# Sliding-window attention feeding a squared-ReLU MLP: three 64-query strips of scores a block instead of four quarters, half blocks of two batches merged, and a new instruction order

## The chip, the cores and the metric

One core of a Trainium2 chip. The time is that of one execution on the device, in microseconds. The engines named below are TensorE (PE, matmuls; its weight loads are shown as PEld), VectorE (DVE), ScalarE (ACT), GpSimd (POOL) and SyncE (SP); the last two, and ACT now and then, also issue DMA transfers.

## The reference

Attention with 8 batches, 8 heads, 576 positions and head size 64. A query sees itself and the 127 positions before it, with a linear bias that depends on the head. The result, as a 4608 x 512 matrix, goes through an MLP of width 2048 with relu squared.

```
B, H, S, D = q.shape                       # 8, 8, 576, 64
window = 128
scores = (q @ k^T) / sqrt(D)
rel = pos[:, None] - pos[None, :]
bias = slopes[h] * -abs(rel)
mask = (rel >= 0) & (rel < window)
scores = where(mask, scores + bias, -1e9)
attn = softmax(scores)
x = (attn @ v) laid out as (B * S, H * D)  # 4608 x 512
h = x @ w_in                               # 512 x 2048
out = relu(h) ** 2 @ w_out                 # 2048 x 512
```

## The kernel before

**Blocks.** A batch's 576 positions are cut into blocks of 128 (`kb` 0 to 3) and a half block of 64 (`kb` 4, `HALF`). `seq` lists the blocks, 40 of them; `ranges` lists 36 column ranges of 128 tokens, where the half blocks of two batches share one. A *job* makes the attention of one or two blocks: six jobs of kind "diag" (`kb` 0: four of a single block, made by `lone`, and two of two blocks), 24 of kind "full" (one block with the block before it) and four of kind "half" (the half blocks of two batches, each with its batch's block 3 before it).

**A full job.** Keys lie on partitions and queries on columns. The scores of a head are two 128 x 128 matmuls over 64 rows of contraction (`pieces`): the block before's keys against the block's queries, and the block's own keys. Heads come in pairs, r = 0 on partitions 0 to 63 and r = 1 on 64 to 127. The 16 matmuls of line 974 fill four PSUM banks of two heads x 256 columns. Four `ACTIVATE` of line 1001 take the exponentials of 512 columns each into a buffer `Pt` (three of them, tag "P"), laid out [128 keys, 8 heads, 2 parts, 128 queries]. Four products of line 1009 on DVE multiply with `masks`, which hold the bias's exponential and zeros outside the window. So of each 256 x 128 window of keys and queries all four quarters of 64 queries are computed, the parts outside the window too. Then `values` multiplies: for each half of the heads eight matmuls of line 1089 (4 heads x 2 parts, 65 columns: 64 of v and one of ones for the sum), a reciprocal (line 1108), and a normalisation (line 1117) into a buffer of x. A DMA transpose on SP (line 1127) puts x into `xT`.

**A half job.** Each of the two half blocks is loaded (lines 854 and 859: k, q and v, 64 rows each) into buffers of its own, transposed by its own DMA transpose on SP (line 900), and has its own 16 score matmuls of 64 columns. The unused half of key rows is zeroed where a buffer is used first (`zero`, line 787). The four exponentials and the four products (line 1016) cover both blocks. Then each block has its own 16 PV matmuls, two reciprocals and two normalisations of 64 rows.

**The MLP.** Tokens go in nine groups of 512. The first product is line 1241 for groups 0 to 2 (`unit`), line 1259 for groups 3 to 5 (`fc_step`) and line 1340 for groups 6 to 8, which use seven products of half-size blocks instead of eight. Relu is line 1202 on ACT, squaring line 1214 on DVE or line 1212 on ACT. The second product is line 1416 for group 0 and line 1503 for the rest, again with seven products (`product`, p = 1 to 7), whose sums of operands DVE makes (`prepare`, line 1633). Outputs are stored by DMA from SP.

**Order.** Nothing here is ordered by dependence alone. Every step is a `Task` with a key, costs and dependencies; `Plan.order` goes through them with a model of engines, buffers and transfers and writes out one fixed order per engine. `ADJ` adds a number to the key of nearly every task, and `SLACK` and the `lat` and `dma` arguments say how late the plan counts on a transfer. The order is fixed before the program runs, so an engine that waits for something holds up all that stands behind it. The rings of buffers ("kq" 4, "v" 9, "kqT" 7, "P" 3, "x" 6, four PSUM banks "a") set how far steps can run ahead.

The plan gives a full job's scores this cost, and the loop over heads is this:

```
t = plan.add({"PE": 213.0 + len(grps) * 2 * len(pieces) * mm(128 if n == 128 else 64)}, due - 32, scores, ...
for c0, w, part, mk, mq in pieces:
    for r in range(2):
        rows = slice(64 * r, 64 * r + 64)
        nc.tensor.matmul(sS[2 * g2 + r].tile[:, jj * 256 + c0:jj * 256 + c0 + w],
                         tile_of(s_kqT[mk])[rows, c, :], tile_of(s_kqT[mq])[rows, C + c, 0:w], ...)
```

Of the kernel before, what the change touches and what calls it, by code (L numbers as in the profile page):

```python
# [11 lines left out]
AF = mybir.ActivationFunctionType  # L12
# [14 lines left out]
SLACK = {"kq": 0.0, "kqT": 4500.0, "v": 2000.0, "x": 2500.0}  # L27
# [11 lines left out]
G_STR = 1  # L39
G_A = 8  # L40
# [14 lines left out]
    "S1.1.0": 6358.822602, "S1.1.1": 6898.050375, "S1.2.0": 10041.2788363, "S1.2.1": 8169.065299, "S1.3.0":  # L55
    10013.995535, "S1.3.1": 8382.076385, "S1.4.0": 17801.930821, "S1.4.1": 15031.337, "S1.5.0": 17384.9929746,
    "S1.5.1": 20260.6174285, "S1.6.0": 22555.8403789, "S1.6.1": 21998.8655, "S1.7.0": 20043.5527584, "S1.7.1":
    25127.1329917, "S1.8.0": 25946.836, "S1.8.1": 26588.9614497, "S2.1.0": 4101.7175, "S2.1.1": 6358.118102,
    "S2.2.0": 8496.8719291, "S2.2.1": 10040.2218363, "S2.3.0": 13560.1077472, "S2.3.1": 12657.244, "S2.4.0":
    16530.7475695, "S2.4.1": 17130.93, "S2.5.0": 17756.8905682, "S2.5.1": 18438.1734398, "S2.6.0":  # L60
    23791.1643648, "S2.6.1": 22459.22941, "S2.7.0": 25315.958184, "S2.7.1": 24765.864872, "S2.8.0":
    24647.825372, "S2.8.1": 26728.7553177, "S3.1.0": 7691.34905, "S3.1.1": 5640.9850318, "S3.2.0": 9443.1491067,
    "S3.2.1": 8550.2682395, "S3.3.0": 10012.235035, "S3.3.1": 13110.8827156, "S3.4.0": 17415.1131664, "S3.4.1":
    18868.3965004, "S3.5.0": 16780.7561245, "S3.5.1": 19805.6045037, "S3.6.0": 22056.5286414, "S3.6.1":
    22074.9870258, "S3.7.0": 25314.861684, "S3.7.1": 26475.2942403, "S3.8.0": 24251.003782, "S3.8.1":
    28098.8773389, "S4.1.0": 6868.250375, "S4.1.1": 7190.2430892, "S4.2.0": 18682.0508077, "S4.2.1":
    18759.5925752, "S4.3.0": 16445.569448, "S4.3.1": 12628.3175, "S4.4.0": 16501.5050695, "S4.4.1":
    14245.0103734, "S4.5.0": 18363.1661199, "S4.5.1": 18363.1046199, "S4.6.0": 22239.6313394, "S4.6.1":
    20124.3504497, "S4.7.0": 26035.141, "S4.7.1": 24736.958872, "S4.8.0": 24185.8589207, "S4.8.1":
    26559.0364497, "b0": 100510, "b1": 100646.465, "b2": 100667.43, "b3": 100715.863, "c11.6.0": 18332.2568341,  # L70
    "c11.6.1": 19590.2485357, "c11.6.2": 21992.696259, "c11.6.3": 19462.4798324, "c11.7.0": 22016.1567401,
    "c11.7.1": 24935.5551633, "c11.7.2": 24734.8259005, "c11.7.3": 23120.6715, "c11.8.0": 26072.1522676,
    "c11.8.1": 26386.3929546, "c11.8.2": 24734.034331, "c11.8.3": 24615.9810863, "c11_1": 4307.4524817, "c11_2":
    8422.0862025, "c11_3": 14308.2115, "c11_4": 17422.5279746, "c11_5": 20884.9988781, "c11_6": 22886.3042408,
    "c11_7": 25714.9587071, "c11_8": 26289.7634823, "c12.6.0": 17228.9717667, "c12.6.1": 18740.1705159,
    "c12.6.2": 23047.354399, "c12.6.3": 25227.0637252, "c12.7.0": 21920.6848572, "c12.7.1": 20046.3418068,
    "c12.7.2": 26385.7442101, "c12.7.3": 21830.9803572, "c12.8.0": 21690.5237178, "c12.8.1": 24263.1766392,
    "c12.8.2": 22834.1277424, "c12.8.3": 24959.2783489, "c12_1": 4613.490023, "c12_2": 13092.42675, "c12_3":
    17664.7600933, "c12_4": 17114.3773214, "c12_5": 22247.0763394, "c12_6": 23129.1952857, "c12_7":
    26163.0233491, "c12_8": 27958.2748967, "c21.0.0_8": 24932.018008, "c21.1.0_8": 26617.6848177, "c21.1.128_8":  # L80
    24928.082008, "c22.6.0": 17468.542771, "c22.6.1": 22092.8820972, "c22.6.2": 22129.5325649, "c22.6.3":
    21949.9206161, "c22.7.0": 21925.0530715, "c22.7.1": 25171.6485544, "c22.7.2": 24892.6130205, "c22.7.3":
    26804.1028891, "c22.8.0": 24693.1109434, "c22.8.1": 25047.3577759, "c22.8.2": 26343.5233117, "c22.8.3":
    27112.1616464, "c22_1": 4337.716, "c22_2": 9783.687498, "c22_3": 11828.507, "c22_4": 17129.2863214, "c22_5":
    22020.5445824, "c22_6": 24970.1156274, "c22_7": 28091.4763389, "c22_8": 27264.6796621, "ck0": 9000458,
    "cq0": 9000504, "dist0": 100701.629, "dist1": 9000167, "e0.0": 100865.465, "e0.1": 100982.763, "e1.0":
    100912.829, "e1.1": 100971.528, "e10.0": 6024.8369206, "e10.1": 6023.9689206, "e10.2": 5839.0722412,
    "e10.3": 5838.2427412, "e11.0": 8333.0698163, "e11.1": 5840.1446162, "e11.2": 11096.131875, "e11.3":
    6021.8962956, "e12.0": 8273.2926913, "e12.1": 9520.9182666, "e12.2": 8282.49653, "e12.3": 8270.2366913,
    "e13.0": 13841.648643, "e13.1": 8283.554405, "e13.2": 11150.984125, "e13.3": 12454.1255232, "e14.0":  # L90
    8210.136138, "e14.1": 8787.0007703, "e14.2": 9519.8080166, "e14.3": 9466.008375, "e16.0": 8885.7162151,
    "e16.1": 8884.6537151, "e16.2": 10342.0834936, "e16.3": 10693.54, "e17.0": 8885.8656867, "e17.1":
    11233.30575, "e17.2": 12129.232199, "e17.3": 12189.03225, "e18.0": 15565.7505509, "e18.1": 15564.6630509,
    "e18.2": 12189.933125, "e18.3": 8882.9630617, "e19.0": 15661.0022219, "e19.1": 12190.774, "e19.2":
    11232.1335, "e19.3": 12188.795, "e2.0": 100934.863, "e2.1": 100993.562, "e20.0": 13016.628, "e20.1":
    14291.5031517, "e20.2": 15562.071875, "e20.3": 15561.406875, "e21.0": 11975.2805813, "e21.1": 13721.9226948,
    "e21.2": 11976.1653893, "e21.3": 15413.6828378, "e22.0": 14172.4779017, "e22.1": 14182.1584369, "e22.2":
    14418.4875177, "e22.3": 14169.3539017, "e24.0": 14226.6730813, "e24.1": 14727.898453, "e24.2":
    15627.3818759, "e24.3": 14602.2, "e25.0": 16482.863696, "e25.1": 13955.27798, "e25.2": 18313.139696,
    "e25.3": 14180.2126869, "e26.0": 14656.6730692, "e26.1": 18194.2829996, "e26.2": 13834.5302836, "e26.3":  # L100
    15828.1824093, "e27.0": 16758.2565536, "e27.1": 15940.2024397, "e27.2": 19504.1119452, "e27.3":
    15938.2764397, "e28.0": 15322.144554, "e28.1": 17988.7125373, "e28.2": 17767.8699853, "e28.3": 15319.004554,
    "e29.0": 15790.0544683, "e29.1": 15788.4093405, "e29.2": 15320.067929, "e29.3": 15786.4843405, "e3.0":
    101062, "e3.1": 101120.698, "e30.0": 15672.7835671, "e30.1": 17466.9708932, "e30.2": 18063.8736786, "e30.3":
    15666.3157155, "e32.0": 19352.6183651, "e32.1": 15668.3965905, "e32.2": 18682.2837426, "e32.3":
    17356.0710976, "e33.0": 18654.8004269, "e33.1": 15203.5509286, "e33.2": 15202.6409286, "e33.3":
    20451.1293954, "e34.0": 15669.9384683, "e34.1": 19765.183, "e34.2": 21275.2451008, "e34.3": 21274.3261008,
    "e35.0": 18534.8561769, "e35.1": 18461.4868024, "e35.2": 20490.0989946, "e35.3": 20336.2020638, "e36.0":
    19373.2814934, "e36.1": 20514.3671669, "e36.2": 20332.1955204, "e36.3": 23191.326944, "e37.0": 18603.768303,
    "e37.1": 21299.7554555, "e37.2": 24035.5923691, "e37.3": 24034.7217238, "e38.0": 21208.26042, "e38.1":  # L110
    24045.6924324, "e38.2": 24871.760639, "e38.3": 19778.8989624, "e4.0": 103407.667, "e4.1": 103466.365,
    "e4.2": 103513.063, "e4.3": 103559.762, "e6.0": 103674.667, "e6.1": 103733.365, "e6.2": 103780.063, "e6.3":
    103826.762, "e8.0": 5554.0984829, "e8.1": 7285.886, "e8.2": 5552.1759829, "e8.3": 5551.0879829, "e9.0":
    5928.4081491, "e9.1": 6031.827125, "e9.2": 6738.730625, "e9.3": 8390.4300663, "ev0.0.0": 100713.333,
    "ev0.0.2": 100713.333, "ev0.1.0": 100759.333, "ev0.1.2": 100785.733, "ev1.0.0": 100757.965, "ev1.0.2":
    100757.965, "ev1.1.0": 100780.298, "ev1.1.2": 100784.364, "ev2.0.0": 100713.43, "ev2.0.2": 100713.43,
# [481 lines left out]
def kernel(  # L598
# [23 lines left out]
    for b in range(0, B, 2):  # L622
        for x in [(b + i, kb) for i in range(2) for kb in range(1, HALF)]:
            jobs.append(("full", [len(seq)]))
            seq.append(x)
            ranges.append([x])
        jobs.append(("half", [len(seq), len(seq) + 1]))
        seq += [(b, HALF), (b + 1, HALF)]

        ranges.insert(len(ranges) - (b + 2 == B), seq[-2:])  # L630
# [1063 lines left out]
```

## Time and profile before

| | |
|---|---|
| median of 3 runs | 299.22 us (297.59 to 299.52) |
| the profiled execution's own time | 299.3 us |
| its span, first to last instruction | 297.4 us |
| mean granted TensorE clock | 1.00 |
| PE / PEld busy | 285.0 / 224.4 us |
| DVE / ACT / POOL busy | 244.0 / 205.8 / 106.3 us |
| line 974, scores of full, half and two-block diag jobs | 544 matmuls |
| line 1001, their exponentials | 120, 63.8 us, mean 604 ns |
| line 1089, PV | 576 matmuls |
| line 900, DMA transposes of q and k on SP | 32, median issue 1342 ns |
| DMA engines | 90% busy or more in the first 28 of 40 slices (to 208 us) |

A busy PE in this profile is one that has matmuls in flight; the matmul's mean duration (273 ns for 256 columns) holds the way through the array as well, so neighbours overlap and the rate is read from the distance of their starts. The chain that ended last is a list of pieces in order of time: start, length, engine and line, number of instructions. A wait is put down to what ended it.

### The profile page before, as it was taken

What the parts mean: (1) busy time and instruction counts of PE and PEld (TensorE: products, weight loads), DVE (VectorE), ACT (ScalarE), POOL (GpSimd) and SP (SyncE); (2) the same over time, 40 slices, a digit from 0 to 9 for tenths busy, and PEclk for the clock granted to TensorE, in tenths of its full rate; (3) what the DMA queues carried; (4) which work ended last, traced back from release to release, by engine and by line L of the source; (5) the groups of instructions that cost most, each with busy time, mean ns of one, the idle gap of its engine ahead of it and who ended that gap; (6) DMA issues with size and microseconds to landing.
All of it is one profiled execution on the core that took longest, in us unless ns stands there. A gap on an engine that the chain in (4) does not pass through costs nothing.

```text
span 297.4 us, 8313 instructions
## 1 busy us (share of the span) xinstructions
PE 285.0 (96%) x3279; PEld 224.4 (75%) x3299; DVE 244.0 (82%) x626; ACT 205.8 (69%) x392; POOL 106.3 (36%) x132
## 2 busy tenths in 40 slices
PE   7899999999998999899999999999999999999994
PEld 3588757888887986457656756768889888888884
DVE  5566568689976996689958997999999998799964
ACT  2785555495496655877679797878999578989600
POOL 8944488452842755441439622710000000000000
PEclk9999999999999999999999999999999999999999
DMA  9999999999999999999999999998212111201124
GB/s 125 168 201 207 184 180 173 155 157 174 163 165 186 161 146 182 158 165 139 155 186 150 148 191 169 165 130 171 68 40 79 53 35 37 71 2 35 31 77 144
DMA packets 170792, 39.62 MB, mean 133 GB/s; under 512 B 156800, under 2 KB 170240, under 8 KB 170752
## 3 DMA queue, kind: packets, MB, share of 16 engines
q0 software_dynamic: 115184, 18.10, 88.9%
q1 hardware_dynamic: 54768, 20.33, 40.0%
q10 hardware_dynamic: 800, 0.66, 0.8%
q8 instruction: 26, 0.43, 0.6%
q14 instruction: 14, 0.11, 0.1%
HBM read 36.70 MB, written 9.44 MB: 155 GB/s over the span
## 4 chain that ended last, share of the span: by engine, by line
PE 69%; DMA 14%; DVE 6%; POOL 4%; issue 3%; ACT 1%; SPq 0%; POOLq 0%; DVEq 0%
PE o L1503 25%; PE h L1259 12%; PE h L1340 10%; PE h L1241 8%; DMA vt<-in_v_dram 5%; PE o L1416 5%; DMA w_out_sb<-in_moe_w_out_dram 4%; PE pv L1089 4%; PE s L974 4%; DMA kqT<-kq 3%; DMA xT<-x 3%; POOL kq L854 2%; POOL vf L859 1%; DVE g L1214 1%; POOL w_in_sb L799 1%
## 5 line engine op out<-in xcount | busy, mean ns | idle before, releaser
L1202 ACT ACTIVATE rt<-h 128x512 bf16<-128x512 f32 (+1 forms) x109 | 64.8, 597 | 32.8 <-PE h L1241 13.9
L1001 ACT ACTIVATE P<-s 128x512 bf16<-128x512 f32 x120 | 63.8, 604 | 7.8 <-PE s L974 7.7
L1503 PEld LDWEIGHTS <-g 128*128 128x128 bf16 x624 | 59.9, 98 | 8.4
L1214 DVE TENSOR_TENSOR g<-rt 128x512 bf16<-128x512 bf16 (+1 forms) x100 | 41.4, 417 | 20.0 <-ACT rt L1202 18.6
L854 POOL DMA_DIRECT2D kq<-in_k_dram x39 | 33.1, 849 | 66.0 <-DMA kqT<-kq 60.7
L1503 PE MATMUL o<-w_out_sb,g 128*128 128x256 bf16 x384 | 47.5, 273 | 0.0
L1241 PE MATMUL h<-xT,w_in_sb 128*128 128x128 bf16 (+1 forms) x512 | 46.2, 246 | 1.0 <-DMA xT<-x 0.9
L1259 PE MATMUL h<-xT,w_in_sb 128*128 128x512 bf16 x178 | 45.5, 379 | 0.7
L1241 PEld LDWEIGHTS <-w_in_sb 128*128 128x128 bf16 x512 | 38.7, 98 | 5.2 <-issue 1.1
L1009 DVE TENSOR_TENSOR P<-P,masks 128x512 bf16<-128x512 bf16 x96 | 38.4, 417 | 2.5 <-ACT P L1001 0.7
L854 POOL DMA_DIRECT2D kq<-in_q_dram x39 | 33.3, 853 | 7.4 <-PE h L1241 3.1
L1117 DVE TENSOR_TENSOR x<-pv,rec 128x256 bf16<-128x256 f32 (+1 forms) x80 | 32.2, 416 | 0.9
L1503 PE MATMUL o<-wsum,sums 128*128 128x256 bf16 x256 | 31.6, 273 | 1.1 <-DVE osb L1561 0.6
L859 POOL DMA_DIRECT2D vt<-in_v_dram x32 | 27.0, 858 | 11.6 <-PE pv L1089 9.8
L1503 PE MATMUL o<-wsum,g 128*128 128x256 bf16 x240 | 29.8, 273 | 0.1
L1089 PEld LDWEIGHTS <-P 128*128 128x128 bf16 x576 | 24.0, 98 | 7.2 <-issue 2.0
L1259 PEld LDWEIGHTS <-w_in_sb 128*128 128x128 bf16 x192 | 16.9, 97 | 15.9
L1212 ACT ACTIVATE g<-rt 128x512 bf16<-128x512 bf16 x45 | 27.9, 629 | 1.1
L1503 PEld LDWEIGHTS <-sums 128*128 128x128 bf16 x256 | 24.4, 98 | 4.8 <-DVE sums L1633 0.6
L1361 DVE TENSOR_TENSOR vf<-h,vf 128x512 f32<-128x512 f32 x36 | 24.1, 683 | 0.8 <-ACT vf L708 0.4
L1202 ACT ACTIVATE rt<-vf 128x512 bf16<-128x512 f32 x36 | 22.2, 624 | 2.4 <-DVE vf L1361 2.2
L1089 PE MATMUL pv<-vt,P 128*128 128x65 bf16 x448 | 22.0, 193 | 1.3 <-DMA vt<-in_v_dram 1.3
(81 smaller groups left out, 382.0 us busy)
## 6 DMA issues: line engine op xcount, KB each, us to landing
out_dram<-osb SPq DMA_DIRECT2D x53, 128.0 KB, 3.8
kq<-in_k_dram POOLq DMA_DIRECT2D x31, 128.0 KB, 7.6
kq<-in_q_dram POOLq DMA_DIRECT2D x31, 128.0 KB, 7.9
vt<-in_v_dram POOLq DMA_DIRECT2D x24, 128.0 KB, 8.0
w_out_sb<-in_moe_w_out_dram POOLq DMA_DIRECT2D x4, 512.0 KB, 14.7
w_in_sb<-in_moe_w_in_dram POOLq DMA_DIRECT2D x3, 512.0 KB, 10.7
vf<-in_v_dram POOLq DMA_DIRECT2D x8, 128.0 KB, 6.9
out_dram<-osb SPq DMA_DIRECT2D x4, 256.0 KB, 6.4
```

Source lines behind the costliest of these rows:

```text
L854: nc.gpsimd.dma_start(view(kq[s_kq[m].idx], i), source(src, m, split))
L859: nc.gpsimd.dma_start(tile_of(s_v[m])[0:n, :, 0:D], source(v, m))
L1001: nc.scalar.activation(flat(Pt[sP.idx]), sS[i].tile.rearrange("p (j t) -> p j t", j=2)[:, :, lo:hi], AF.Exp, bias=0.0, scale=scale)
L1009: nc.vector.tensor_tensor(flat(Pt[sP.idx]), flat(Pt[sP.idx]), flat(masks), op=ALU.mult)
L1089: nc.tensor.matmul(sv.tile[0:full, hi * (D + 1):(hi + 1) * (D + 1)], prob, tile_of(s_v[mk])[:, h, 0:D + 1], start=mk == parts[0][1], stop= ...
L1117: nc.vector.tensor_tensor(o, heads(sv)[rows, :, 0:D], sr.tile[rows, :].unsqueeze(2).to_broadcast([n, 4, D]), op=ALU.mult)
L1202: nc.scalar.activation(srt.tile[:, 0:n], i, AF.Relu, bias=0.0, scale=1.0)
L1214: nc.vector.tensor_tensor(o, i, i, op=ALU.mult)
L1241: nc.tensor.matmul(slot.tile[:, f * w:(f + 1) * w], w_in_sb[:, cc, fc * 128:(fc + 1) * 128], xT[:, cc, lo % (XR * 128):lo % (XR * 128) + w ...
L1259: nc.tensor.matmul(slot.tile, w_in_sb[:, cc, fc * 128:(fc + 1) * 128], xT[:, cc, g * 512 % (XR * 128):g * 512 % (XR * 128) + 512], start=c ...
L1340: nc.tensor.matmul(slot.tile[:, j * 256:j * 256 + 256], a, b_, start=fresh and j == 0 and c == 0, stop=c == 1, skip_group_check=True)
L1503: nc.tensor.matmul(slot.tile[:, z * 256:z * 256 + 256], stationary(c), moving(c), start=fresh and z == 0 and c == 0, stop=c == F - 1, skip ...
```

## The change

Scores of a full block are now three strips of 64 queries per head. Strip one is the block before's 128 keys against the early 64 queries, strip two the block's own 128 keys against the late 64 queries. The third strip holds two 64 x 64 tiles on top of each other: the block's early keys with its early queries on partitions 0 to 63, and the block before's late keys with its late queries on partitions 64 to 127. The quarter that is left out in each part lies wholly outside the window. Two PSUM banks per r hold 512 and 256 columns. Exponentials are taken of these, 512 and 256 columns twice. Of the four mask products, the odd ones read the third strip once for each of the two quarters that it belongs to and multiply with masks whose other half is zero.

The half blocks of two batches are one block of 128 rows: one entry in `seq` (36 instead of 40), one kq buffer, one transpose, one key block for PV. Its scores are again two strips from 128 keys and one from 64 x 64 tiles. The exponentials lie in one P buffer, and a second one, `sR`, holds the late queries' share of the second batch's earlier block, with zeros (`clear`, `far_late`, `far_early`, `near`) where batch and query do not belong together. PV takes three parts a head and 128 queries at once.

Heads are laid out in P as even heads, then odd heads (`place`), as the single-block jobs had them. The plan's numbers for transfers and for the scores change (`S_PE`, `lat`, `SLACK`, `dma`), a few dependencies are added, and all of `ADJ` is replaced.

```diff
-SLACK = {"kq": 0.0, "kqT": 4500.0, "v": 2000.0, "x": 2500.0}
+SLACK = {"kqT": 4500.0, "v": 2300.0, "x": 2700.0}
+S_PE = 375.0
 ADJ = {
...
-        jobs.append(("half", [len(seq), len(seq) + 1]))
-        seq += [(b, HALF), (b + 1, HALF)]
+        jobs.append(("half", [len(seq)]))
+        seq.append((b, HALF))
...
     def place(h):
-        return (h // 4) * 4 + (h % 2) * 2 + (h // 2) % 2
+        return (h % 2) * 4 + h // 2
...
-    def zero(m, tag, slot, key, part, after):
...
+                    for rows, from_ in sources(src, m):
+                        nc.gpsimd.dma_start(view(kq[s_kq[m].idx], i)[rows], from_)
+            t_kq[m] = [plan.add({"POOL": 1780.0 * parts}, key, fetch_kq, [], [s_kq[m]], dma=2 * ns,
+                                name=f"lkq{m}", count=2 * parts, lat=2800.0 if m >= N_PE else None)]
...
         if kind == "full":
+            banks = [[(mb, whole, 0, early), (me, whole, 64, late)], [(me, early, 0, early), (mb, late, 0, late)]]
+        elif kind == "half":
+            banks = [[(mk, whole, 64 * i, (early, late)[i]) for i, mk in enumerate(before)],
+                     [(me, early, 0, early), (me, late, 0, late)]]
...
+                todo = [(n, c, p) for n, pieces in enumerate(banks) for c in range(C) for p in pieces]
+                for n, c, (mk, keys, at_c, qs) in todo:
+                    mq = mk if diag else me
+                    for half in (keys,):
+                        for r in range(2):
+                            rows = slice(64 * r, 64 * r + 64)
...
+                                w = (128, 64)[n]
+                                o = sS[2 * r + n].tile[half, c * w + at_c:c * w + at_c + 64]
+                            nc.tensor.matmul(o, tile_of(s_kqT[mk])[rows, c, half],
+                                             tile_of(s_kqT[mq])[rows, C + c, qs], start=True, stop=True)
...
+            t = plan.add({"PE": 213.0 + (449.0 if diag else S_PE)}, due - 32, scores,
...
+        sP, sR = Slot("P"), Slot("P")
...
+            cols = 256 if i % 2 and not diag else 512
...
+                if i % 2:
+                    nc.vector.tensor_tensor(p[:, :, 1:3], p[:, :, 2:3].to_broadcast([128, 4, 2, 64]), mk[:, :, 1:3], op=ALU.mult)
+                else:
+                    nc.vector.tensor_tensor(p[:, :, 0:4:3], p[:, :, 0:4:3], mk[:, :, 0:4:3], op=ALU.mult)
...
+        if kind == "half":
+            def clear():
+                nc.vector.memset(Pt[sR.idx][:, :, 0, early], 0.0)
+            def far_late():
+                nc.vector.tensor_tensor(Pt[sR.idx][:, :, 0, late], Pt[sP.idx][:, :, 0, late], masks[:, :, 0, early],
+                                        op=ALU.mult)
+            def far_early():
+                p = Pt[sP.idx][:, :, 0, early]
+                nc.vector.tensor_tensor(p, p, masks[:, :, 0, early], op=ALU.mult)
+                nc.vector.memset(Pt[sP.idx][:, :, 0, late], 0.0)
+            def near(w):
+                p = Pt[sP.idx][:, w, 1].rearrange("p c (s q) -> p c s q", s=2)
+                nc.vector.tensor_tensor(p, p[:, :, 1:2].to_broadcast([128, 4, 2, 64]),
+                                        masks[:, w, 1].rearrange("p c (s q) -> p c s q", s=2), op=ALU.mult)
+                nc.vector.memset(Pt[sP.idx][early, w, 1, late], 0.0)
...
+            parts = [(s, slice(0, 128), mk) for s, mk in zip((sP, sR), before)] + [(sP, slice(128, 256), m)]
...
-                      need + wneed + [st.get(("P", p, 0))] + ([st[after]] if after else []),
+                      need + wneed + [st.get(("P", p, 0)), st["P", 2, 1] if p == 5 else None] + ([st[after]] if after else []),
...
+        built = t_mask[0] + t_mask[1] + t_bias if g == 0 else []
```

## The prediction

> **What bounds the kernel now.** I read the engine totals first, then what TensorE (PE) waits for, then the chain that ended last, then the instructions of single score stages in the timeline, and last the groups by shape.
>
> ```profile
> PE 285.0 (96%) x3279; PEld 224.4 (75%) x3299; DVE 244.0 (82%) x626; ACT 205.8 (69%) x392; POOL 106.3 (36%) x132
> ```
>
> PE is busy for 285.0 of 297.4 us. The 12.4 us without it lie mostly at the start: before 20 us the list of PE's waits holds 3.5 us, and from 20 us on some 3.8 us:
>
> ```profile
> PE pv L1089 <- DMA vt<-in_v_dram: 1.3, 1, 1.3
> ...
> PE h L1241 <- DMA xT<-x: 0.9, 1, 0.9
> PE o L1503 <- DVE osb L1561: 0.6, 2, 0.4
> ```
>
> So the time is the sum of PE's stream, and an edit counts by what it does to that stream or to these few waits. A score stage can be priced in the chain (start, length, instructions), where each piece runs from the end of the piece before:
>
> ```profile
> 143.13 0.97 PE pv L1089 x32
> ...
> 202.53 0.87 PE o L1503 x8
> 203.40 0.55 PE s L974 x16
> 203.96 0.98 PE h L1340 x8
> ...
> 220.54 0.57 PE s L974 x32
> 221.11 0.54 PE h L1340 x4
> ```
>
> A full block's 16 score matmuls take 0.55 us. The eight 256-column matmuls behind them take 0.98 us, where eight take 0.87 elsewhere. So a stage costs 0.55 + 0.11 = 0.66 us. A half job's 32 take 0.57 us, and the four behind them 0.54 against 0.44 in other pieces: 0.67 us. The timeline shows what fills it:
>
> ```profile
> 203.68 0.22 PE L974 MATMUL s<-kqT,kqT 64*128 64x128 bf16 x2
> 203.74 0.22 PE L974 MATMUL s<-kqT 64*128 64x128 bf16 x2
> ...
> 220.83 0.22 PE L974 MATMUL s<-kqT,kqT 64*128 64x64 bf16 x4
> 220.89 0.22 PE L974 MATMUL s<-kqT 64*128 64x64 bf16 x4
> ```
>
> Two matmuls of 64 rows (heads r = 0 and 1, lower and upper half of the array) go side by side: a pair of 128 columns every 0.057 us, two pairs of 64 columns every 0.06, so 0.03 a pair. Eight pairs of 0.057 are 0.45, sixteen of 0.03 are 0.48. What is left, 0.10 us, is the step from 128-row to 64-row tiles; the step back is the 0.11 seen above, put at 0.10 below. PV matmuls run at 0.97/32 = 0.03 us each.
>
> **Scores (line 974).** A full block now issues 16 matmuls of 64 columns for the first two strips (8 pairs, 8 x 0.03 = 0.24 us), and then 16 in 64x64 tiles for the third. With both steps a stage is 0.10 + 0.24 + S + 0.10 = 0.44 + S, where S is the third strip. No row shows a matmul with fewer than 128 weight columns, so S is bounded. Low: the four quarters of the array run side by side as two halves do now, and the step into 64x64 tiles is free: 4 x 0.03 = 0.12. High: the 16 run one after another and the step costs as much as the one from 128 rows: 16 x 0.03 + 0.10 = 0.58. Between them lie four at a time with a step (0.22), and pairs without and with a step (0.24 and 0.34). I take four at a time, since row halves already start together, and half a step, since the row split stays and only the columns are split: S = 0.17, stage 0.61. Against 0.66 that saves 0.05 us x 24 blocks = 1.2 us (bounds: gain 2.4, loss 8.6). For the four half jobs the new stage is the same 0.61 against 0.67: 0.06 x 4 = 0.2 us (bounds: gain 0.4, loss 1.4).
>
> [...]
>
> **PV (line 1089).** A half job had two blocks x 8 heads x 2 parts = 32 matmuls. It now has 8 x 3 = 24 (two earlier key blocks, and one merged own block): 8 x 0.03 x 4 jobs = 1.0 us off PE. Full blocks keep 16; the new head order changes no count.
>
> **Exponentials (line 1001).** Four of 512 columns become two of 512 and two of 256. From the groups by shape (busy us, mean ns of one, idle before):
>
> ```profile
> L1001 ACT ACTIVATE P<-s 128x512 bf16<-128x512 f32 x120 | 63.8, 604 | 7.8 <-PE s L974 7.7
> ...
> L1009 DVE TENSOR_TENSOR P<-P,masks 128x512 bf16<-128x512 bf16 x96 | 38.4, 417 | 2.5 <-ACT P L1001 0.7
> ...
> L1117 DVE TENSOR_TENSOR x<-pv,rec 64x256 bf16<-64x256 f32 x16 | 6.6, 418 | 0.3
> ...
> L1202 ACT ACTIVATE rt<-h 128x256 bf16<-128x256 f32 x2 | 0.8, 387 | 0.0
> ```
>
> The nearest row for 256 is 387 ns, so two of them save 0.43 us a job: 12 us of ACT over 28. I cost this at nothing. ACT is 69% busy and PE's list shows 0.4 us behind these exponentials; were that cover gone, a block's masks would start 0.4 us earlier.
>
> **Masks (lines 1009, 1016).** Full blocks keep four products of 512. Two of them spread the third strip over two quarters; the half job's old product (line 1016) already read masks in repeated runs of 64 at 415 ns, so 417 stands. A half job keeps four products and gains four fills: two as the old zero fill of v (272 ns) and two near that of kqT (165 ns), 0.9 us. It loses two of four reciprocals (line 1108, 171 ns) and two of four normalisations (418 ns): 1.2 us. With three old zero fills gone (2 x 272 + 165 ns), DVE is lighter by 4 x 0.3 + 0.7 = 1.9 us. It lies beside PE, so nothing. The wait is longer, though: PV of a half job now stands behind three products and two fills, about 1.3 us against one product. Behind PV in PE's queue stand MLP products that need none of it, placed by the order; uncovered, that is 4 x 1 = 4 us.
>
> **Loads, SP, buffers.** A half job's loads stay four for q and k and two for v, now in one task each. Its two transposes (line 900) become one: four fewer on SP at 1.34 us, beside PE. It holds one kq and one kqT buffer instead of two, but two of three P buffers: the next block's exponentials may wait, up to a stage's 2 us of ACT, which PE covers with products. Product 5's new dependency is implied by its bank, which product 2 holds first. `built` is empty for every group that calls `prepare`.
>
> **Order.** All keys are new, and so are landing times: loads counted 0.4 us longer, v's margin 0.3 and x's 0.2 us larger. The two DMA waits, 1.3 + 0.9 = 2.2 us, are where a later place of the reader can gain. Bounds: all 3.8 us gone, or as many new ones, loss 3.8. I take half of the two, a gain of 1.1 us.
>
> **Sum.** 1.2 + 0.2 + 1.0 + 1.1 = 3.5 us. The profiled execution took 299.3 us (its span and 1.9 us around it); the median of the runs is 299.2. So 299.3 - 3.5 = 295.8 us, 1.2% below, just over the 1% that a measurement of this kernel can tell from no change.
>
> **Rivals.** (1) The step into 64x64 tiles costs its full 0.10 and the order returns nothing: S = 0.22, the stage as long as before, PV's 1.0 us alone: 298.3 us. For it: every change of tile shape in this trace costs 0.09 to 0.11. Against it: the row split stays.
>
> (2) Slower, in the third strip: its matmuls do not overlap, because each small weight load stands in front of its matmul. S = 0.58, the stage 1.02: 24 x 0.36 + 4 x 0.35 = 10 us lost, 1.0 gained, so 308.3 us. It decides from S = 0.26 on, where 28 x 0.04 eats PV's gain. For it: no row has such loads. Against it: in the half job two 128-column loads pass every 0.03 us. Four abreast with loads half hidden gives S near 0.4: 24 x 0.18 + 4 x 0.17 - 1.0 = 4 us, 303.3. [...]
>
> (3) The order turns against PE: DMA is at 90% or more of its time until 208 us, and v or x late for one or two readers, at 7 us from issue to landing, adds waits like the 1.3 us one. Four more, or the half jobs' uncovered PV, eat the gain and 2.5 us: 301.8.
>
> (4) The mask that repeats a quarter drops to the rate of the 683 ns rows: 48 x 0.27 = 13 us more DVE, which from 160 to 240 us is busy 9.6 us or more in seven of eight windows of 10; a third on the path is 4 us, so 300.5 after the gains.
>
> **Chances.** Forecast 0.47 (own range 293 to 297.5), (1) 0.28, (2) 0.12, (3) 0.08, (4) 0.05. Under 296.2: 0.40 from the forecast and 0.05 from (1) with a kinder order, 0.45. Over 302.2: 0.11 of (2), 0.04 of (3) and 0.02 of (4), 0.17. The rest, 0.38, is within 1%. The range runs from 292.0 (low S, all waits gone, 299.3 - 2.8 - 1.0 - 3.8 = 291.7) to 302.5, which leaves out 0.05 below and 0.13 above.
>
> **What would show it.** The timeline of a full block's scores: 16 matmuls at 0.03 a pair, then sixteen 64x64 ones within 0.12 to 0.22 us, and 0.10 before and after. ACT busy near 194 us, DVE near 242 us, PE busy near 283 us, PV matmuls 544 instead of 576, and PE's list without the two DMA waits. A third strip over 0.26 us, masks above 500 ns, or new PE waits over 3 us in sum prove it wrong.

## The result, and the profile after

The changed kernel took 301.6 us in the median (20 runs, 298.39 to 305.75), the kernel before 299.16 us beside it (20 runs, 297.32 to 301.02). The ratio is 1.0062 [1.0035, 1.0089]: slower by 0.6%, where 1.2% less time was forecast. The ratio leaves out executions more than 1.5% above the fastest, six of the changed kernel's 20; with them the medians differ by 0.8%.

Two executions of the changed kernel were profiled. In the first (305.1 us, called A) the granted TensorE clock was 0.50 for 6.8 us, so the page is read from the second (301.9 us, span 300.1, called B). Its engine totals:

```profile
PE 286.3 (95%) x3651; PEld 224.4 (75%) x3651; DVE 237.7 (79%) x621; ACT 196.3 (65%) x394; POOL 106.2 (35%) x132
```

ACT is 9.5 us lighter than before and DVE 6.3, as the change meant; PE, which sets the end, is no lighter. The 285.0 us of before are a little low, since 20 of its 3299 matmul records are missing. The run below in which two of before's four exponentials are cut has the same PE work and all records:

```profile
PE 286.8 (97%) x3299; PEld 225.1 (76%) x3299; DVE 243.9 (82%) x629; ACT 195.4 (66%) x392; POOL 106.3 (36%) x132
```

So PE's busy time is about the same before and after. Its list of waits in B (us in total, times, longest):

```profile
PE pv L1119 <- DMA vt<-in_v_dram: 3.0, 1, 3.0
PE h L1280 <- DMA xT<-x: 2.6, 2, 1.6
```

The two DMA waits of before, 1.3 and 0.9 us, have become 3.0 and 2.6. The chain of B shows the longer one (start, length, what):

```profile
194.94 13.39 DMA vt<-in_v_dram
208.32 0.04 issue
208.36 0.61 PE pv L1119 x15
...
210.29 0.59 PE s L975 x32
210.88 0.98 PE h L1361 x8
```

The v of block 32 (batch 7) is issued at 194.94 and lands 13.4 us later. PE stands at the first PV that reads it. Below that, a score stage is 0.59 for its 32 matmuls and 0.11 more than usual in the eight behind them: 0.70 us here. Another measure is the distance from the start of the last matmul ahead of a stage to the start of the first behind it, less one usual distance of 0.109 us. Its median over the stages that stand between matmuls of 256 columns is 0.684 after, against 0.650 (full) and 0.669 (half) before. The timeline of one full stage tells why:

```profile
150.62 0.20 PE L975 MATMUL s<-kqT,kqT 64*128 64x64 bf16 x2
150.66 0.19 PE L975 MATMUL s<-kqT 64*128 64x64 bf16 x2
...
150.83 0.34 PE L975 MATMUL s<-kqT 64*128 64x64 bf16 x4
150.96 0.22 PE L975 MATMUL s<-kqT,kqT 64*64 64x64 bf16 x2
151.01 0.20 PE L975 MATMUL s<-kqT 64*64 64x64 bf16 x2
151.01 0.20 PE L975 MATMUL s<-kqT,kqT 64*64 64x64 bf16 x2
```

A pair of the first two strips goes every 0.03 us. The row at 150.83 holds the last of those pairs and, since it is 0.34 long, one pair of 64x64 tiles that starts with the row at 150.96. The next pair was due at 150.83 + 0.03 = 150.86. So the step from 64x128 to 64x64 tiles is 150.96 - 150.86 = 0.10 us. From there the 64x64 tiles start in rounds of four (two rows with one start, as at 151.01): the first takes 0.05, the others 0.03 each.

What landed later is seen in the rows of DMA issues (issues, KB each, median us to landing). Before:

```profile
kq<-in_q_dram POOLq DMA_DIRECT2D x31, 128.0 KB, 7.9
vt<-in_v_dram POOLq DMA_DIRECT2D x24, 128.0 KB, 8.0
```

and B:

```profile
kq<-in_q_dram POOLq DMA_DIRECT2D x31, 128.0 KB, 10.3
vt<-in_v_dram POOLq DMA_DIRECT2D x24, 128.0 KB, 11.7
```

The bytes are nearly the same (39.62 and 39.65 MB). It goes with the order, not with this execution: every trace of the new order with all its stores has a median of 9.4 us or more in the three 128 KB rows of k, q and v, and the two of the old order have at most 8.3. What in the order brings it is not shown.

Execution A has the same wait, 3.1 us, and then this (windows: stretch, its length, PE busy, PEld, DVE, ACT, POOL, PEclk, DMA share, GB/s):

```profile
205.00:209.00 4.00, 0.90 (x12) 0.74 (x10) 1.20 (x4) 0.00 (x0) 0.00 (x0) 0.87 1.58 134
209.00:213.00 4.00, 4.00 (x50) 2.89 (x51) 1.72 (x5) 1.11 (x3) 0.00 (x0) 0.50 0.93 272
...
216.00:220.00 4.00, 4.00 (x39) 3.59 (x37) 4.00 (x9) 3.50 (x8) 0.00 (x0) 1.00 0.06 16
```

PE goes idle at 205.8 us. From 208.0 us on, 2.2 us into the wait, the granted clock is 0.50, for 6.8 us in all; at 216 us it is full again. In A PE is busy for 289.7 us, 3.4 more than in B. B had no such drop: its mean clock of 0.997 comes from the end of the span alone, where the clock is 0.50 from 298.5 us on and PE's last matmul is over at 295.8. B's page shows it only in the last of 40 slices:

```profile
PEclk9999999999999999999999999999999999999998
```

### The profile page after: what moved, and what is told of

The parts are those of the page before. It is cut to its first block, busy times and chain, and to the rows that moved or that the text cites. A ratio compares the mean times of both kernels' runs of the same rounds, so it can differ in the third digit from the quotient of the medians.

```text
span 303.3 us, 9031 instructions
## 1 busy us (share of the span) xinstructions
PE 289.7 (96%) x3651; PEld 226.6 (75%) x3651; DVE 238.1 (78%) x621; ACT 196.4 (65%) x394; POOL 106.2 (35%) x132
## 2 busy tenths in 40 slices
DMA packets 170665, 39.65 MB, mean 131 GB/s; under 512 B 156672, under 2 KB 170112, under 8 KB 170624
## 4 chain that ended last, share of the span: by engine, by line
PE 68%; DMA 21%; POOL 5%; DVE 3%; issue 1%; ACT 0%; POOLq 0%; DVEq 0%
PE o L1524 25%; PE h L1361 12%; PE h L1280 9%; PE h L1262 9%; DMA xT<-x 6%; DMA w_in_sb<-in_moe_w_in_dram 5%; DMA vt<-in_v_dram 4%; PE s L975 4%; PE o L1437 4%; PE pv L1119 3%; DMA kq<-in_q_dram 3%; DMA kqT<-kq 3%; POOL kq L853 2%; POOL vf L859 1%; POOL w_in_sb L794 1%; DVE sums L1653 1%
## 5 line engine op out<-in xcount | busy, mean ns | idle before, releaser
L1008 ACT ACTIVATE P<-s 128x512 bf16<-128x512 f32 (+1 forms) x120 | 51.7, 503 | 16.5 <-PE s L975 16.3
L1235 DVE TENSOR_TENSOR g<-rt 128x512 bf16<-128x512 bf16 (+1 forms) x105 | 43.6, 419 | 22.4 <-ACT rt L1223 21.2
L1524 PE MATMUL o<-w_out_sb,g 128*128 128x256 bf16 x384 | 48.9, 276 | 0.0
L713 ACT ACTIVATE osb<-o 128x512 f32<-128x512 f32 x25 | 14.8, 597 | 26.7 <-PE o L1524 22.5
L1119 PEld LDWEIGHTS <-P 128*128 128x128 bf16 x544 | 23.2, 98 | 8.0 <-issue 3.9
L1143 DVE TENSOR_TENSOR x<-pv,rec 128x256 bf16<-128x256 f32 x72 | 28.4, 415 | 0.6
L1233 ACT ACTIVATE g<-rt 128x512 bf16<-128x512 bf16 x40 | 25.2, 630 | 1.2
L1119 PE MATMUL pv<-vt,P 128*128 128x65 bf16 x416 | 21.0, 194 | 3.1 <-DMA vt<-in_v_dram 3.1
```

Source lines behind the costliest of these rows:

```text
L1008: nc.scalar.activation(o, s, AF.Exp, bias=0.0, scale=scale)
L1119: nc.tensor.matmul(sv.tile[:, hi * (D + 1):(hi + 1) * (D + 1)], prob, tile_of(s_v[mk])[:, h, 0:D + 1], start=mk == parts[0][2], stop=mk == m)
L1143: nc.vector.tensor_tensor(o, heads(sv)[:, :, 0:D], sr.tile.unsqueeze(2).to_broadcast([n, 4, D]), op=ALU.mult)
L1233: nc.scalar.activation(o, i, AF.Square, bias=0.0, scale=1.0)
L1235: nc.vector.tensor_tensor(o, i, i, op=ALU.mult)
L1524: nc.tensor.matmul(slot.tile[:, z * 256:z * 256 + 256], stationary(c), moving(c), start=fresh and z == 0 and c == 0, stop=c == F - 1, skip ...
```

## The experiments

The theory after the result: PE's own work came out even, and the order's late loads, above all block 32's v, cost the time. The rivals: the step into 64x64 tiles costs it (undo the step), the half clock behind the wait costs it (fill the wait), or ACT's relief is worth something that the order hides.

**The changed kernel again.** The reference for what follows.

> The changed kernel once more, for a profile with the full clock throughout. Theory W (the loss is waits of PE for transfers in the new order): PE's list again shows 5 us or more behind DMA vt<-in_v_dram and DMA xT<-x after 100 us, 3.8 us at most being there before. Theory S (the loss is the longer score stages): these waits are about as before, 2 to 3 us. Time 299 to 302 us under both.

302.05 us (8 runs, 299.38 to 304.76), before beside it 300.06 (24 runs); ratio 1.0057 [1.0007, 1.0107]. Its profile is B.

**No step: every score strip from 64x64 tiles.**

```diff
-                    for half in (keys,):
+                    for half in ((early, late) if keys == whole and not diag else (keys,)):
```

> All scores of full and half jobs from 64x64 tiles, so that a stage has no second step of the tile shape. Same order. Rounds of four at 0.031 us: 12 x 0.031 plus 0.10 before and 0.10 behind plus 0.02 for the first loads, 0.59 us against 0.68 for 28 stages, 2.6 us less PE work. Theory S: the time falls by that, to about 298.4 us. Theory W: the order's waits stay and take part of it back, since PE comes sooner to loads that land when they land: 299.5 to 300.5 us.

305.19 us (4 runs), ratio 1.0187 [1.0131, 1.0242]. The stage did fall, to 0.602 us, which is 28 x 0.08 = 2.3 us less PE work. The waits for the late vt and xT are still there (2.4 and 1.8 us). But PE now also waits for nothing that the profile can name:

```profile
PE o L1524 <- issue: 3.4, 4, 1.5
PE s L975 <- issue: 1.4, 1, 1.4
PE h L1262 <- issue: 0.8, 1, 0.8
```

These 5.6 us are more than the step cost. The timeline shows the longest, 0.3 us behind a score stage (in brackets the idle time):

```profile
74.01 0.28 PE L1524 MATMUL o<-wsum,sums 128*128 128x256 bf16 x1
75.78 0.93 PE L1524 MATMUL o<-wsum,sums 128*128 128x256 bf16 x7 [1.49 <-issue]
```

The queue of kind "instruction" offers a reading. In B, and then in this kernel, its row reads:

```profile
q8 instruction: 28, 0.46, 0.7%
```

```profile
q8 instruction: 32, 0.52, 0.7%
```

Each packet is 16,384 bytes. Before has 26 of them for 6598 PE instructions (3299 loads and as many matmuls), B 28 for 7302, this kernel 32 for 8198: one for 254, 261 and 256 PE instructions. The author's reading of this count is that the queue brings PE's program; no run shows it directly. In the trace a packet starts at 72.84, 81.31 and 88.82 us, and the three longest stalls before 100 us end at 75.78, 83.79 and 91.64, 2.5 to 2.9 us later. An all-64x64 stage puts 96 instructions into 0.5 us; by the reading, two or three near one another use up what one packet brought before the next has come. The next runs test it.

**The loads of block 32's and block 35's v change places on POOL.** In the changed order block 35's v is issued ahead of block 32's, though it is read some 30 us later (in B the two are read at 208.4 and 238.1 us). All other engines' orders stay.

```diff
     done = plan.order()
+    i, j = (next(n for n, t in enumerate(done) if t.name == x) for x in ("lv32", "lv35"))
+    done[i], done[j] = done[j], done[i]
+    s_v[32].idx, s_v[35].idx = s_v[35].idx, s_v[32].idx
```

> Only the places of two loads of v on POOL are swapped: block 32's (issued last, needed first) and block 35's (the last half block, needed 25 us later). The order on every other engine stays. Theory W: the wait of 3.1 us for vt near 206 us and the half clock after it go, and the time falls by 2 to 4 us to 297 to 299 us. Theory S: another reader waits in its place, 300.5 to 301.5 us.

297.55 us (8 runs), before 300.06: ratio 0.9924 [0.9881, 0.9967], and 4.5 us below the changed kernel beside it. The span is 293.7, and all of PE's waits are those of the start:

```profile
PE wm L882 <- DVE sums L731: 1.2, 1, 1.2
PE s L1076 <- ACT kqf L713: 0.8, 1, 0.8
PE pv L1119 <- ACT kqf L713: 0.6, 1, 0.6
PE tp L913 <- ACT kqf L713: 0.2, 1, 0.2
```

PE is busy 286.5 us, as in B. So the loss does not lie in PE's work, but in the waits and what follows them. The xT waits are gone too; but the loads of this execution were 3.7 us ahead of B's already at 117 us (the same v goes out at 113.6 instead of 117.3), which a swap of loads after 180 us can't have caused. For the vt wait the swap is the cause: none of the seven profiles with it (this one and those of the six swapped kernels below) has this wait, and all four with the old places and all stores have it, 1.3 to 3.1 us, also the one where PE filled 2.7 us of it.

**Both edits.**

> Both edits. Theory W: the gain of the swap and 1 to 2 us of the shorter stages, 295 to 297 us, below the kernel before. Theory S: 298 to 299 us.

302.86 us (10 runs), ratio 1.0102 [1.0067, 1.0137]. No vt wait is left, but "issue" waits of 2.6 (line 1524) and 1.4 us (line 975). The stalls do not hang on the late load, and the time lies above what either theory expected.

**The third strip twice, loads swapped.** As many instructions as in the no-step kernel, with the step left in.

```diff
+                if not diag:
+                    todo += [x for x in todo if x[0] == 1]
```

> On the kernel with the swapped loads (297.6 us): each matmul of the third strip is issued twice, which adds 16 matmuls and 16 weight loads to each of 28 stages and leaves 64x128 tiles as they are. Theory F (when 64 scores were all made from 64x64 tiles, PE ran out of fetched instructions: 96 in half a microsecond): the stage grows by 0.13 us, 3.5 us in all, and waits for issue of 1 us and more come up in PE's list again, 3 us or more in sum, so 303 us or more. Theory T (it was the tile shape or the earlier arrival at transfers): no such waits, 300 to 301.5 us.

305.92 us (4 runs), ratio 1.0208 [1.011, 1.0307], some 8 us above the swapped kernel. The stage is 0.81 us, 28 x 0.126 = 3.5 us of PE work; 5.1 us more are "issue" waits again, at the same three kinds of places (3.2, 1.0 and 0.9 us), with 32 packets on q8 again. So they come with the step left in, too. The two kernels share their 32 packets and their stages of 96 instructions, which speaks for number and density. But both also have more 64x64 matmuls a stage than B (48 and 32 against 16), and no run adds instructions of another shape to the stages. The shape is thus not ruled out, though most of these stalls stand ahead of other lines than the scores'.

**The 256-column exponentials twice, loads swapped.**

```diff
-                nc.scalar.activation(o, s, AF.Exp, bias=0.0, scale=scale)
+                for _ in range(2 if i % 2 and not diag else 1):
+                    nc.scalar.activation(o, s, AF.Exp, bias=0.0, scale=scale)
```

> On the kernel with the swapped loads: each exponential of 256 columns is issued twice, 56 more at 0.39 us, 22 us more ACT, about twice what the change took away. If ACT's relief is hidden, as forecast at nothing: 297.5 to 299 us. If exponentials stand on the path of the score and PV stages: 301 us or more, with PE waiting for P or for PSUM.

300.85 us (8 runs), ratio 1.0076 [1.0035, 1.0117]: 2.5 to 3.3 us above the swapped kernel's two medians (297.55 and, below, 298.37) for 18 us of ACT (196.3 to 214.4). PE now waits for ACT by name, here and there:

```profile
PE h L1362 <- ACT rt L1224: 0.6, 1, 0.6
PE h L1281 <- ACT rt L1224: 0.4, 2, 0.2
PE pv L1120 <- DVE P L1026: 0.3, 1, 0.3
```

These waits are short, and more of the kind lies in PE's busy time, which rises from 286.5 to 289.3 us, since a gap shorter than a matmul in flight (273 ns on average at 256 columns, where B's usual distance from start to start is 109) does not show. About a sixth of what is added to ACT reaches the end, between "all hidden" and what a bound on ACT would give.

**The wait filled.** The changed order, with 48 matmuls of 128 columns on a constant ahead of the late PV.

```diff
+                for _ in range(48 if (m, hf) == (32, 0) else 0):
+                    nc.tensor.matmul(sv.tile[:, 0:128], ident, ident, start=True, stop=True)
```

> The changed kernel with 48 idle matmuls of 128 columns (2.7 us) ahead of the PV stage that waits for block 32's v, so that PE is busy while it waits. Theory: the half clock in some executions is set off by that idle stretch of 3 us. Then the wait itself is filled and costs what it did, the mean clock is 1.00 in the profiled execution, and the time is 300 to 301.5 us with no execution over 303. If the clock falls for another reason: executions at 304 and 305 us as before.

300.87 us (10 runs), ratio 1.0053 [1.0016, 1.0091], highest 302.49. The clock stayed up: its mean is 0.997 or more in all 10 executions, which the end of the span alone can give, as in B. Of the changed kernel's 28 it is 0.994 or less in 17, with a median of 302.7 us, and 0.997 or more in 11, with 300.1; of before's 70 in the three series of runs it is that low in 5, and of the swapped kernel's 20 in 3. So here the idle stretch sets off the half clock (0 of 10 executions with it filled, 17 of 28 without). The executions with it are 2.6 us slower in the median, and the spread up to 305.75 goes with it. The wait itself, which no filling shortens, keeps the median above before's.

**The third strip from 64x128 tiles, loads swapped.** No step, but two exponentials of 64 partitions instead of one of 128.

```diff
-                            nc.tensor.matmul(o, tile_of(s_kqT[mk])[rows, c, half],
+                            nc.tensor.matmul(o, tile_of(s_kqT[mk])[rows, c, :],
...
+                    for t, ks in enumerate((early, late)):
+                        nc.scalar.activation(o[ks], s[ks, :, t], AF.Exp, bias=0.0, scale=scale)
```

> On the kernel with the swapped loads: the third strip is made from 64x128 tiles too (all 128 keys against 64 queries, the half that is not wanted is not read), with no step into 64x64 tiles, and two exponentials of 64 partitions in place of one of 128. 8 pairs at 0.03 instead of a step of 0.09 and four rounds: 0.67 us a stage against 0.68, 0.4 us less on PE in all; ACT gets 56 more of 0.39 us. If the 64x64 tiles are worth nothing on PE: 297 to 298.5 us. If they are worth what I forecast (0.05 us a stage): 299 us or more.

304.08 us (4 runs), ratio 1.0175 [1.0132, 1.0218]. The stage is 0.669, hardly below 0.684, and ACT rises to 219.1 us, since half the partitions take about as long, 375 ns against 390 for 128 partitions in the swapped kernel:

```profile
L1011 ACT ACTIVATE P<-s 64x256 bf16<-64x256 f32 x112 | 42.0, 375 | 1.1
```

PE waits for ACT's rt 2.7 us in all, and PE's busy time rises to 289.2 us, as with the doubled exponentials. The expectation had counted the 56 more of ACT and given them no price: on this kernel the 64x64 tile saves an exponential, not PE time.

**The swapped kernel in more runs.**

> The kernel with the two loads of v swapped once more, in five rounds, to be compared within this job: 297 to 298.5 us, below the kernel before.

298.37 us (12 runs), before 298.73 (29 runs): ratio 0.9974 [0.9938, 1.0009]. One comparison has it 0.8% below before, this one 0.3% with an interval that reaches 1. It is better than the changed kernel; that it beats before is not settled.

**All 64x64 in some stages only, loads swapped:** in the stages of blocks 8, 9 and 17 to 28, chosen because PE's other work there has few instructions a microsecond.

```diff
+ALL64 = {8, 9} | set(range(17, 29))
...
+                    for half in ((early, late) if keys == whole and ms[0] in ALL64 else (keys,)):
```

> The swapped loads, and all scores from 64x64 tiles in 14 of the 28 stages: blocks 8, 9 and 17 to 28, where PE's other work of that time has few instructions a microsecond. If fetching is what made 28 such stages slow, there are no waits for issue above 0.5 us here and the stages save 14 x 0.08 = 1.1 us: 296 to 297 us. If stages of 64x64 tiles cost time in another way, half of that loss shows: 300 us or more.

299.64 us (12 runs), ratio 1.0034 [1.0003, 1.0064], where 296 to 297 had been expected. In the profile a single stall of 2.5 us, which ends at 153.1 us in a score stage and 3.4 us after a packet of q8 started, took more than the 14 x 0.08 = 1.1 us that the stages saved. So this choice of stages did not avoid the stalls, and the reading does not yet tell where one comes.

**Before, with two of four exponentials cut to 256 columns.** The masks and PV read the values that the cut leaves out as they lie in the buffer.

```diff
-                nc.scalar.activation(flat(Pt[sP.idx]), sS[i].tile.rearrange("p (j t) -> p j t", j=2)[:, :, lo:hi],
+                at = lo if kind == "diag" or i % 2 == 0 else lo + 128
+                nc.scalar.activation(flat(Pt[sP.idx])[:, :, at - lo:], sS[i].tile.rearrange("p (j t) -> p j t", j=2)[:, :, at:hi],
```

> The kernel before, in its own order, with two of the four exponentials of each full and half job cut from 512 to 256 columns, as the change has them (the first key block's weights of four heads are then stale; 0.8 us of fills at the start are added). ACT loses 12 us. By my forecast this is worth nothing: 299 to 300 us. By the rate at which doubled exponentials cost time (4 us for 22): 2 us less, 297 us.

298.87 us (12 runs), ratio 1.0003 [0.9978, 1.0029], with ACT at 195.4 us. The relief by itself is worth nothing that can be told, 0.3% either way.

**The changed order with fewer output stores:** 30 of 53 issues of 128 KB from osb left out and 4 of 16 of 64 KB, 4.2 MB in all; loads not swapped. Those rows of the output are not written.

```diff
-                    for r, at_p, n in rows_of(4 * g + tok + j):
+                    for r, at_p, n in rows_of(4 * g + tok + j) if g > 4 else []:
```

> The changed kernel, loads not swapped, without the output stores of groups 1 to 4 (those rows are not written; 4.2 MB less for the DMA engines, most of it before 210 us). If the pace of the DMA engines sets when block 32's v lands, the wait near 206 us shrinks below 1 us and the time comes to 297 to 299 us. If the load is late because POOL issues it late, for want of a buffer: the wait stays near 3 us and the time at 301 to 302 us.

295.84 us (4 runs), ratio 0.9894 [0.9858, 0.993]. This is more than 1 us below what was expected where the DMA engines' pace sets the wait. The last v is issued at 189.2 instead of 194.9 us, and neither vt nor xT is waited for. The same order with less for the DMA engines to move has no late reader.

## Why the prediction was wrong

Its range held the time, its sign did not. Point by point:

- **Scores: the failed term is S**, put at 0.17 us, measured 0.684 - 0.44 = 0.24. The four tiles do go side by side, a round of four every 0.03 us in B. But the "half a step, since the row split stays" is a whole one, 0.10 us, and the first round of the new tiles takes 0.02 longer than the others. Where 1.2 and 0.2 us were to be gained, 24 x 0.034 + 4 x 0.015 = 0.9 us are lost.
- **PV**: 544 matmuls, 32 x 0.03 = 1.0 us less, as forecast. With the scores, PE's work is the same as before. Rival (1), with S = 0.22, had the step right; it lacked the 0.02 of the first round in each stage, and it had no new waits.
- **Order: the second failed term.** Forecast was half of 2.2 us of DMA waits gone, -1.1. The vt wait grew by 1.7 and the xT wait by 1.7; three small waits of before (0.6 for osb, 0.4 for P, 0.4 for w_out) went: +2.0 us. Together 0.9 - 1.0 + 2.0 = 1.9 of the 2.7 us by which B's span is longer (300.1 - 297.4). Another 0.4 us stands behind PE's last matmul (4.3 us to the end of the span, 3.9 before); the remaining 0.4 us is open. The half clock has no part in B; in the median it has, and the prediction did not have it. The waits are rival (3)'s mechanism with two readers instead of four. The prediction's row "7 us from issue to landing" was taken as a constant of the kernel; in B the medians of its 128 KB loads of k, q and v are 9.4 to 11.7, and block 32's v took 13.4. (The DMA engines of before are at 90% or more in the first 27 slices of 40, to 201 us, not to 208.)
- **The step the sum lacked** lies in the fixed order itself: on the POOL queue, block 35's v stands ahead of block 32's. The prediction argued about the sum of waits where it should have compared, load by load, the order of issue with the order of need.
- **Exponentials at nothing**: right as far as can be told. ACT fell to 196.3 (forecast 194), and the cut alone gave 1.0003. It holds for relief only: ACT made heavier costs about a sixth of what is added, so its cover is not wide.
- **Masks**: 417 and 415 ns (lines 1025 and 1023). Rival (4) did not come.
- **DVE, fills, half job's PV behind three products**: DVE is 6.3 us lighter (forecast 1.9), and PE waits for no product of it. Nothing on the path, as said.
- **Rival (2)**, a third strip that does not overlap, decided from S = 0.26 on. S is 0.24, and its cause is the step, not the overlap: a round of the new tiles takes 0.03 us, as a pair of 64x128 tiles does, and only the first takes 0.05.
- **What was to prove it wrong**: new PE waits of over 3 us in sum. They came, +3.4 us at two places.
- **Where PE is idle**: the prediction put the 12.4 us without PE mostly at the start. Of them 3.9 us stand behind PE's last matmul, and about 1 us is only the missing records.

Open: why one execution's transfers run some 3 us ahead of another's with the same order up to there, and so what the xT waits cost by themselves and how much of the swapped kernel's advantage over before is lasting.

## What to carry to other kernels

Price each change of tile shape as a full step, whichever side of the tile changes (here 0.10 us from 128-row to 64-row tiles, and 0.10 from 64x128 to 64x64), and ask on which engine the new shape really saves: here one exponential for two on ACT, which had time to spare. When an order changes, compare for each queue the sequence of its loads with the sequence in which they are read; one load behind another that is needed 30 us later cost 0.8 to 1.3% of the time (1.0057 against 0.9974 and 0.9924), 2.5 to 4 us, about what the whole edit was to bring (3.5). And before splitting matmuls on a busy PE, count instructions as well as cycles: the three kernels with 8198 PE instructions lost 4.0 to 5.6 us to stalls.

## What the runs showed of the hardware that was not expected

- In four kernels PE stood still for 0.4 to 2.6 us at a time with no wait that the profile can name. These stalls end 2.3 to 3.4 us after a packet of 16,384 bytes of q8 starts. By the author's reading PE had then run out of instructions. The count fits it (32 packets for 8198 instructions, with 96 instructions of a stage in 0.5 us), and so do all four kernels; but no run changed the fetch itself, so this stays a reading.
- The granted clock fell to 0.50 after short idle stretches of PE: in A 2.2 us into a wait of 3.1, for 6.8 us. In the profiles of the no-step kernel, of both edits and of the kernel with 14 such stages it is 0.50 for 3.4 us, from at most 1 us behind a wait or stall of 2.4 to 2.6 us. B's wait of 3.0 us had no such drop, and in none of the 10 executions with the filled wait does the mean clock point to one. So the length of a wait alone does not decide here.
- In B four 64x64 tiles ran at once: a round of four 64-column matmuls went every 0.03 us, the same as a pair of 64x128 tiles.
